# First chunks as fp32 on two other queues, loads ahead of the weights, and a new instruction order, in a windowed attention and highway kernel

## The chip, the cores and the metric

The kernel runs on one core of one Trainium2 chip. The metric is the time of one execution on the device in microseconds (us); a time "of runs" is a median over several executions, and a "span" is the length of one traced execution, some 1.7 us shorter than its run. A difference counts as a change if it is over 2%. The engines are named as the profile names them: PE is TensorE's matmuls and PEld its weight loads, DVE is VectorE, ACT ScalarE, POOL GpSimd, SP SyncE.

## The reference, cut to what matters

```python
# q, k, v: [4, 8, 768, 64] fp32; n_sink = 4, window = 128
scores = q @ k.transpose(0, 1, 3, 2) / sqrt(64)
keep = (column < n_sink) | (0 <= row - column < window)
a = softmax(where(keep, scores, -1e9)) @ v          # [4, 8, 768, 64]
x = a.transpose(0, 2, 1, 3).reshape(3072, 512)
H = maximum(x @ w_h, 0);  T = sigmoid(x @ w_t + b_t)
out = T * H + (1 - T) * x                           # [3072, 512] fp32
```

## The kernel before

The 3072 tokens are 24 blocks of 128, six to a batch. Block n needs query chunk n, key and value chunks n-1 (of its batch), n and n+1 (the chunks are cut 64 rows apart from the blocks), the four sink keys of its batch, and both weight matrices. Its steps have short names in one long list that fixes the order on every engine:

```python
"Tq": transpose of a query chunk (TensorE)     "tq"/"tqV": its copy out of PSUM (ScalarE / VectorE)
"Tk", "tk": the same for a key chunk           "S": scores, "x0_", "x1_": exponentials (ScalarE)
"m0_", "m1_": masks (VectorE)                  "sk", "es": sink scores and their exponentials
"A": the av matmuls                            "xh": division by the row sums (VectorE)
"X", "xT": transpose of x and its copy         "Mh", "Mt": x @ w_h, x @ w_t;  "u": tanh (ScalarE)
"d", "e", "o": the mix and the output (VectorE)
"fk": fills the sink tiles of batch 0 and the bias row (VectorE)
```

All loads of q, k, v and the weights are issued by GpSimd and cast from fp32 to fp16 on the way. The first lines of its queue, and the place where a later batch's sink keys are copied:

```python
        load_q(0); load_k(0); load_k(1)
        ...                                  # identity
        load_v(0)
        tri(mask, ...)  # x4, the masks
        load_q(1); load_v(1); load_k(2)
        load_w(moe_w_h, wh_sb)
        ...
        load_v(2); load_q(2); load_k(3)
        load_w(moe_w_t, wt_sb)
        load_v(3)
        ...                                  # then q, k, v of one block after the other
    def copy_T(m, g, eng=None):
        ...
        if g and m and m % NSC == 0 and m < NB:
            fill_ks(m // NSC, nc.gpsimd)     # two small copies of the sink keys
            sink_v(m // NSC, nc.gpsimd)
```

The softmax here doesn't subtract the row's maximum and nothing guards it: scores larger than these inputs give would overflow.

Of the kernel before, what the change touches and what calls it, by code (L numbers as in the profile page):

```python
# [20 lines left out]
def kernel(  # L21
# [18 lines left out]
    nc = tc.nc  # L40
# [85 lines left out]
    es_t = [const.tile([P, 2, P], FP16, tag=f"es{i}", name=f"es{i}") for i in range(2)]  # L126

    with tc.manual_schedule(engines={ENG.DVE}):
        nc.vector.memset(k_first[0:HP], 0.0)
        nc.vector.memset(v_ring[0][0:HP, 0:H * 65], 0.0)  # L130
        nc.vector.memset(warm, 0.0)
        nc.vector.memset(ident, 1.0)
        nc.vector.memset(ebias, _EXP_BIAS)
        nc.vector.memset(mask, 1.0)
        nc.vector.memset(bm, 1.0)
        for vt in v_ring:
            init_v(vt)
        nc.vector.memset(bt16, 0.0)
        nc.vector.memset(ones_row, 0.0)
        nc.vector.memset(ones_row[0:1, :], 1.0)  # L140
        for i in range(2):
            nc.vector.memset(ks_bd[i], 0.0)
            nc.vector.memset(vs_bd[i], 0.0)
            nc.vector.memset(es_t[i], 0.0)
# [11 lines left out]
    def load_w(w, sb):  # L156
        nc.gpsimd.dma_start(out=sb, in_=w.rearrange("(kc p) of -> p kc of", p=P))

    with tc.manual_schedule(engines={ENG.Pool, ENG.SP}):
        nc.sync.dma_start(out=bt32, in_=moe_b_t.unsqueeze(0))  # L160
        for b in range(B):
            nc.sync.dma_start(out=vs_dn[b], in_=v[b, :, 0:NSINK, :])
        load_q(0)
        load_k(0)
        load_k(1)
        nc.gpsimd.affine_select(
            out=ident, in_=ident, compare_op=ALU.is_equal, fill=0.0,
            base=0, pattern=[[-1, P]], channel_multiplier=1)
        load_v(0)
        tri(mask, slice(0, HP), 0, P, HP - 1, -1, 1)  # L170
        tri(mask, slice(HP, P), 0, P, 0, 1, -1)
        tri(mask, slice(0, HP), P, EW, 0, 1, -1)
        tri(mask, slice(HP, P), P, EW, -1, -1, 1)
        load_q(1)
        load_v(1)
        load_k(2)
        load_w(moe_w_h, wh_sb)
        nc.gpsimd.affine_select(
            out=bm, in_=bm, compare_op=ALU.is_ge, fill=0.0,
            base=0, pattern=[[-NSINK, H]], channel_multiplier=1)  # L180
        nc.gpsimd.affine_select(
            out=bm, in_=bm, compare_op=ALU.is_ge, fill=0.0,
            base=NSINK - 1, pattern=[[NSINK, H]], channel_multiplier=-1)
        load_v(2)
        load_q(2)
        load_k(3)
        load_w(moe_w_t, wt_sb)
        load_v(3)


    def more_masks():
        nc.vector.tensor_copy(out=mask0, in_=mask)
        nc.vector.memset(mask0[0:HP, 0:P], 0.0)
        nc.vector.memset(mask0[HP:HP + NSINK, 0:P], 1.0)
        nc.vector.memset(mask0[HP:P, P:EW], 0.0)
# [62 lines left out]
    def act_sink(n):  # L258
        es = es_t[(n if n < NSC else n // 2) % 2]
        bl = sink_blocks(n)  # L260
        nc.scalar.activation(out=es[0:NS4, 0:len(bl)], in_=sk_of.pop(n)[0:NS4, 0:len(bl)],
                             func=AF.Exp, bias=ebias[0:NS4], scale=SCALE)
        for t, m in enumerate(bl):
            es_of[m] = es[:, t, :]
# [38 lines left out]

    def pe_AB(n):
        av = av_ps.tile([P, 2, 4, P], FP32, tag="av", name="av")
        av_of[n] = av
# [98 lines left out]
    TS = 6  # L405
# [43 lines left out]
    def norm(n):  # L449
        dve_rec(n)  # L450
        dve_x(n)

    STEP = {
# [84 lines left out]
```

## Time and profile before

Three runs: 132.74 us median (132.39 to 134.89); the traced run took 130.48 us, with a span of 128.8.

| | busy us | share of the span |
|---|---|---|
| PE | 109.5 | 85% |
| DVE | 102.3 | 79% |
| ACT | 90.7 | 70% |
| POOL | 76.4 | 59% |

The view by stretches adds up each engine's busy time between two times. Columns: stretch in us, its length, then busy us (instructions) of PE, PEld, DVE, ACT, POOL, the granted TensorE clock, the DMA share and GB/s.

```profile
0.00:30.00 30.00, 19.88 (x288) 11.62 (x289) 15.38 (x71) 13.67 (x21) 24.19 (x38) 1.00 1.63 123
30.00:50.00 20.00, 18.09 (x366) 11.54 (x365) 16.15 (x33) 16.02 (x29) 18.12 (x24) 1.00 2.05 173
50.00:126.00 76.00, 71.56 (x1340) 45.43 (x1338) 70.77 (x130) 61.06 (x102) 34.12 (x42) 1.00 1.13 127
```

The reader is to see VectorE: 15.38 of the first 30 us, 16.15 of the next 20, and nearly all of the rest. With the work left as it is, the time can fall here only by what VectorE (and TensorE beside it) stands idle: 26.5 us of the span for VectorE.

### The profile page before, as it was taken

The numbers are of one execution on the slowest core, as the hardware profiler recorded it, in microseconds if no ns is written. First come the engines' busy times: TensorE is split into PE (matmuls) and PEld (weight loads), VectorE is DVE, ScalarE is ACT, GpSimd is POOL, SyncE is SP. The second block draws the span as 40 slices with busy tenths as digits, with TensorE's granted clock in tenths as the row PEclk, the third lists the DMA queues.
The fourth block names the chain that finished last, engine by engine and source line by source line (L and its number), as shares of the span: only waits on it lengthen the run. The fifth ranks groups of instructions, "written<-read, shape, count | busy, mean of one in ns | idle before, by whom it ended". The sixth has DMA issues, their size and how long they took to land.

```text
span 128.8 us, 4699 instructions
## 1 busy us (share of the span) xinstructions
PE 109.5 (85%) x1984; PEld 68.6 (53%) x1984; DVE 102.3 (79%) x232; ACT 90.7 (70%) x150; POOL 76.4 (59%) x102
## 2 busy tenths in 40 slices
PE   4841948979999769997999999999899999999830
PEld 1221735355676346665665665667466665665310
DVE  7618432548996939994999999989999999899990
ACT  3253626448989857999688879989689798893310
POOL 6998965788997898997869996846100000000000
PEclk9999999999999999999999999999999999999997
DMA  0999999999999999999999999999221022211142
GB/s 4 113 72 141 138 178 169 155 144 116 163 207 159 204 169 144 172 159 194 209 178 101 195 181 159 206 200 156 88 87 59 28 87 84 81 48 38 74 153 99
DMA packets 79702, 17.11 MB, mean 133 GB/s; under 512 B 75585, under 2 KB 76609, under 8 KB 79682
## 3 DMA queue, kind: packets, MB, share of 16 engines
q0 software_dynamic: 76064, 10.49, 122.1%
q1 hardware_dynamic: 3618, 6.33, 13.7%
q8 instruction: 15, 0.25, 0.8%
q14 instruction: 5, 0.04, 0.1%
HBM read 21.01 MB, written 6.29 MB: 212 GB/s over the span
## 4 chain that ended last, share of the span: by engine, by line
PE 66%; DVE 10%; POOL 8%; DMA 6%; ACT 4%; issue 4%; POOLq 0%; ACTq 0%
PE hps L377 14%; PE tps L364 13%; PE av L323 6%; DMA v<-in_v_dram 6%; PE av L312 6%; PE xtp L351 5%; PE sps L229 4%; PE sps L272 4%; PE sps L285 4%; PE sk L254 4%; PE tps L362 4%; PE av L329 3%; DVE dd L383 3%; DVE xh L342 2%; POOL v L104 2%
## 5 line engine op out<-in xcount | busy, mean ns | idle before, releaser
L290 ACT ACTIVATE e<-sps,ebias 128x768 f16<-128x768 f32 x48 | 41.3, 895 | 5.9 <-PE sps L285 5.8
L234 ACT COPY t<-sps 128x512 f16<-128x512 f16 x47 | 25.0, 583 | 12.7 <-PE sps L229 12.7
L298 DVE TENSOR_TENSOR e<-e,mask 128x768 f16<-128x768 f16 x48 | 26.0, 565 | 6.1 <-ACT e L290 5.6
L104 POOL DMA_DIRECT2D v<-in_v_dram x28 | 23.6, 841 | 8.1 <-DVE e L298 1.9
L377 PE MATMUL hps<-wh_sb,xT 128*128 128x512 f16 x96 | 25.5, 394 | 0.0
L364 PE MATMUL tps<-wt_sb,xT 128*128 128x512 f16 x96 | 24.6, 379 | 0.0
L97 POOL DMA_DIRECT2D ksd<-in_k_dram x27 | 23.2, 860 | 0.8 <-issue 0.5
L90 POOL DMA_DIRECT2D qsd<-in_q_dram x24 | 22.1, 921 | 2.2 <-DMA wt_sb<-in_moe_w_t_dram 1.3
L370 ACT ACTIVATE u<-tps 128x512 f16<-128x512 f32 x24 | 14.4, 599 | 9.2 <-PE tps L364 7.2
L389 DVE SCALAR_TENSOR_TENSOR ee<-u,dd 128x512 f16<-128x512 f16 x24 | 17.1, 714 | 0.4 <-ACT u L370 0.2
L383 DVE SCALAR_TENSOR_TENSOR dd<-hps,xh 128x512 f16<-128x512 f32 x24 | 16.5, 688 | 1.1 <-PE hps L377 1.0
L342 DVE TENSOR_TENSOR xh<-av,rec 128x512 f16<-128x512 f32 x24 | 16.6, 691 | 0.8
L395 DVE SCALAR_TENSOR_TENSOR otok<-xh,ee 128x512 f32<-128x512 f16 x24 | 16.6, 690 | 0.7
L364 PEld LDWEIGHTS <-xT 128*128 128x128 f16 x96 | 9.3, 97 | 11.7 <-issue 1.3
L312 PE MATMUL av<-v,e 64*64 64x66 f16 x384 | 11.2, 197 | 2.9 <-DMA v<-in_v_dram 2.1
L377 PEld LDWEIGHTS <-xT 128*128 128x128 f16 x96 | 9.5, 102 | 7.9 <-issue 1.6
L272 PE MATMUL sps<-t,t 64*128 64x128 f16 x192 | 12.6, 227 | 1.2 <-ACT t L234 1.2
L356 ACT COPY xT<-xtp 128x512 f16<-128x512 f16 x16 | 9.3, 583 | 3.3 <-PE xtp L351 3.2
L312 PEld LDWEIGHTS <-e 64*64 64x64 f16 x384 | 8.7, 111 | 4.6 <-DVE e L298 2.3
L337 DVE RECIPROCAL rec<-av 128x8 f32<-128x8 f32 x24 | 4.9, 205 | 7.8 <-PE av L329 6.5
L351 PE MATMUL xtp<-ident,xh 128*128 128x128 f16 x96 | 9.9, 227 | 1.3 <-DVE dd L383 0.8
L229 PE MATMUL sps<-ident,ksd 64*128 64x64 f16 x192 | 7.1, 196 | 4.5 <-DMA ksd<-in_k_dram 4.5
(61 smaller groups left out, 132.4 us busy)
## 6 DMA issues: line engine op xcount, KB each, us to landing
out_dram<-otok SPq DMA_DIRECT2D x24, 256.0 KB, 4.8
qsd<-in_q_dram POOLq DMA_DIRECT2D x24, 128.0 KB, 7.4
ksd<-in_k_dram POOLq DMA_DIRECT2D x20, 128.0 KB, 7.2
v<-in_v_dram POOLq DMA_DIRECT2D x20, 128.0 KB, 7.5
v<-in_v_dram POOLq DMA_DIRECT2D x8, 64.0 KB, 6.2
wh_sb<-in_moe_w_h_dram POOLq DMA_DIRECT2D x1, 512.0 KB, 8.1
wt_sb<-in_moe_w_t_dram POOLq DMA_DIRECT2D x1, 512.0 KB, 9.0
ksd<-in_k_dram POOLq DMA_DIRECT2D x7, 64.0 KB, 7.1
```

The lines of the kernel that those rows point to most:

```text
L90: nc.gpsimd.dma_start(out=qsd, in_=q[b, :, c * P:(c + 1) * P, :].transpose([1, 0, 2]))
L97: nc.gpsimd.dma_start(out=ksd[rows], in_=k[b, :, s0:s0 + nr, :].transpose([1, 0, 2]))
L104: nc.gpsimd.dma_start(out=vt[rows, :, 0:D], in_=v[b, :, s0:s0 + nr, :].transpose([1, 0, 2]))
L234: (eng or nc.scalar.copy)(out=t.rearrange("p a (h b) -> p h a b", b=HP), in_=t_view(s_tile(n, g)))
L272: nc.tensor.matmul(sps[:, hh, hl * EW:hl * EW + P], lhsT=kT[n][rows, hp, :], rhs=qT[n][rows, hp, :], start=True, stop=True)
L290: nc.scalar.activation(out=e.rearrange("p a b c -> p a (b c)"), in_=s_tile(n, g)[:, :, 0:2 * EW], func=AF.Exp, bias=ebias, scale=SCALE)
L298: nc.vector.tensor_tensor(out=ev, in0=ev, in1=m.unsqueeze(1).to_broadcast([P, 4, EW]), op=ALU.mult)
L312: nc.tensor.matmul(av[part, h // 4, h % 4, 0:_AVN], lhsT=e_at(n, h)[src, P:EW], rhs=vt[src, 65 * h:65 * h + _AVN], start=(h % 4 == 0), sto ...
L342: nc.vector.tensor_tensor(out=xh.rearrange("p (h d) -> p h d", d=D), in0=av_of.pop(n)[:, :, 0:D], in1=rec_of.pop(n).unsqueeze(2).to_broadc ...
L364: nc.tensor.matmul(tps, lhsT=xT[:, kc, :], rhs=wt_sb[:, kc, :], start=False, stop=(kc == NOC - 1))
L377: nc.tensor.matmul(hps, lhsT=xT[:, kc, :], rhs=wh_sb[:, kc, :], start=(kc == 0), stop=(kc == NOC - 1))
L383: nc.vector.scalar_tensor_tensor(out=dd, in0=h_of.pop(n), scalar=0.0, in1=xh_of[n], op0=ALU.max, op1=ALU.subtract)
```

## The change

Its intent is to have the queries and keys of blocks 0 to 4 and the values of blocks 0 and 1 on the chip before the weights (two matrices of 512 KB in fp16) take the DMA engines, and to use the wait for the weights for the transposes and sink scores of blocks 1 to 4. Five first loads go to SyncE and ScalarE as fp32, uncast, and are converted by VectorE and ScalarE. Cut to its core:

```diff
+        load_f32("q", 0, nc.sync)
+        load_f32("k", 0, nc.scalar)
+        load_f32("k", 1, nc.sync)
+        load_f32("v", 0, nc.scalar)
+        load_f32("v", 1, nc.sync)
         ...
-        load_q(0) load_k(0) load_k(1) ... load_v(0) tri x4 load_q(1) load_v(1) load_k(2)
-        load_w(moe_w_h, wh_sb) ... load_v(2) load_q(2) load_k(3) load_w(moe_w_t, wt_sb) load_v(3)
+        load_q(1) ... load_q(2) load_k(5) ... load_q(3) load_k(2) load_v(2) load_k(3)
+        tri x4  load_q(4) load_k(4)
+        load_w(moe_w_h, wh_sb) load_v(3) load_w(moe_w_t, wt_sb)
+        load_k(6) load_q(5) load_v(4) load_v(5) load_k(7) load_q(6) ...
-    es_t = [... for i in range(2)]
+    es_t = [... for i in range(4)]
     ORDER = """
-    Tq:0 Tk:0 tq:0 tk:0 Tk:1 tk:1 S:0 x0_:0 x1_:0 m0_:0 m1_:0 fk:0 Tk:2 Tq:1 tk:2 A:0 tq:1 xh:0
-    S:1 sk:1 x0_:1 X:0 xTV:0 x1_:1 m0_:1 es:1 m1_:1 A:1 Tq:2 xh:1 Tk:3 tq:2 tk:3 X:1 xT:1 S:2 ...
+    ckV:0 cq:0 ma:0 Tk:0 Tq:0 tk:0 ma:1 ck:1 tq:0 mc:0 Tk:1 tk:1 fk:0 S:0 x0_:0 cvV:0 x1_:0
+    mz0_:0 Tq:1 m0_:0 tq:1 Tq:2 m1_:0 tq:2 Tq:3 cvV:1 tq:3 sk:2 mz1_:0 Tk:2 es:2 Tk:5 tk:2 tkV:5
+    S:1 A:0 x0_:1 sk:1 x1_:1 xh:0 Tk:4 tk:4 m0_:1 Tk:3 es:1 m1_:1 Tq:4 tk:3 sk:3 tqV:4 es:3 sk:4
+    A:1 es:4 X:0 xh:1 S:2 ...
```

"ck", "cq", "cv" are conversions (V: on VectorE), "ma" clears the sink tiles, "mc" the bias rows, "mz0_", "mz1_" make the masks of a batch's first two blocks. The kernel before ran these clears ahead of the list (VectorE was done with them at 5.46 us) and the sink set-up "fk" behind the first block's masks; now the clears stand in the list, and they and "fk" come ahead of the masks. The order from block 20 on is new too, and one constant that says which score tile hosts a transpose goes from 6 to 8. The four sink tiles are needed by the new order: "es:4" now comes before the av of block 2, which still reads what "es:2" wrote, so with two tiles it would be overwritten (worked out from the list).

More of the change, by code (lines that the diff above doesn't have):

```diff
@@ L125, with load_f32, convert @@
     vs_dn = [const.tile([NS4, D], FP32, tag=f"vd{i}", name=f"vd{i}") for i in range(B)]
-    es_t = [const.tile([P, 2, P], FP16, tag=f"es{i}", name=f"es{i}") for i in range(2)]
+    es_t = [const.tile([P, 2, P], FP16, tag=f"es{i}", name=f"es{i}") for i in range(4)]
     with tc.manual_schedule(engines={ENG.DVE}):
+        nc.vector.memset(ident, 1.0)
+        nc.vector.memset(warm, 0.0)
+        nc.vector.memset(mask, 1.0)
+        nc.vector.memset(bm, 1.0)
+        nc.vector.memset(ebias, _EXP_BIAS)
         nc.vector.memset(k_first[0:HP], 0.0)
         nc.vector.memset(v_ring[0][0:HP, 0:H * 65], 0.0)
-        nc.vector.memset(warm, 0.0)
-        nc.vector.memset(ident, 1.0)
-        nc.vector.memset(ebias, _EXP_BIAS)
-        nc.vector.memset(mask, 1.0)
-        nc.vector.memset(bm, 1.0)
         for vt in v_ring:
             init_v(vt)
-        nc.vector.memset(bt16, 0.0)
-        nc.vector.memset(ones_row, 0.0)
-        nc.vector.memset(ones_row[0:1, :], 1.0)
-        for i in range(2):
-            nc.vector.memset(ks_bd[i], 0.0)
-            nc.vector.memset(vs_bd[i], 0.0)
-            nc.vector.memset(es_t[i], 0.0)
+    f32_of = {}
+    def load_f32(kind, n, eng):
+        t = const.tile([P, H, D], FP32, tag=f"{kind}f{n}", name=f"{kind}f{n}")
+        src = {"q": q, "k": k, "v": v}[kind]
+        for rows, b, s0 in ([(slice(0, P), 0, n * P)] if kind == "q" else chunk_parts(n)):
+            nr = rows.stop - rows.start
+            eng.dma_start(out=t[rows], in_=src[b, :, s0:s0 + nr, :].transpose([1, 0, 2]))
+        f32_of[kind, n] = t
+    def convert(kind, n, eng):
+        rows = slice(HP, P) if kind != "q" and n == 0 else slice(0, P)
+        if kind == "v":
+            dst = v_ring[n][:, 0:H * 65].rearrange("p (h e) -> p h e", e=65)[:, :, 0:D]
+        elif kind == "q":
+            dst = q_sd[n] = sd_pool.tile([P, H, D], FP16, tag="qsd", name="qsd")
+        else:
+            dst = k_sd[n] = k_first if n == 0 else sd_pool.tile([P, H, D], FP16, tag="ksd",
+                                                                name="ksd")
+        eng(out=dst[rows], in_=f32_of.pop((kind, n))[rows])
     def tri(t, rows, lo, hi, base, step, cm):
@@ L162 @@
             nc.sync.dma_start(out=vs_dn[b], in_=v[b, :, 0:NSINK, :])
-        load_q(0)
-        load_k(0)
-        load_k(1)
+        load_q(1)
         nc.gpsimd.affine_select(
@@ L168 @@
             base=0, pattern=[[-1, P]], channel_multiplier=1)
-        load_v(0)
-        tri(mask, slice(0, HP), 0, P, HP - 1, -1, 1)
-        tri(mask, slice(HP, P), 0, P, 0, 1, -1)
-        tri(mask, slice(0, HP), P, EW, 0, 1, -1)
-        tri(mask, slice(HP, P), P, EW, -1, -1, 1)
-        load_q(1)
-        load_v(1)
-        load_k(2)
-        load_w(moe_w_h, wh_sb)
+        load_q(2)
+        load_k(5)
         nc.gpsimd.affine_select(
@@ L183, with first_mask @@
             base=NSINK - 1, pattern=[[NSINK, H]], channel_multiplier=-1)
+        load_q(3)
+        load_k(2)
         load_v(2)
-        load_q(2)
         load_k(3)
-        load_w(moe_w_t, wt_sb)
-        load_v(3)
-    def more_masks():
+        tri(mask, slice(0, HP), 0, P, HP - 1, -1, 1)
+        tri(mask, slice(HP, P), 0, P, 0, 1, -1)
+        tri(mask, slice(0, HP), P, EW, 0, 1, -1)
+        tri(mask, slice(HP, P), P, EW, -1, -1, 1)
+        load_q(4)
+        load_k(4)
+        load_w(moe_w_h, wh_sb)
+        load_v(3)
+        load_w(moe_w_t, wt_sb)
+        load_k(6)
+        load_q(5)
+        load_v(4)
+        load_v(5)
+        load_k(7)
+        load_q(6)
+        load_v(8)
+        load_k(8)
+        load_q(7)
+        load_v(7)
+        load_v(6)
+    def first_mask(_):
         nc.vector.tensor_copy(out=mask0, in_=mask)
@@ L195, in more_masks, with second_mask, clear_sinks, bias_rows @@
         nc.vector.memset(mask0[HP:P, P:EW], 0.0)
+    def second_mask(_):
         nc.vector.tensor_copy(out=mask1, in_=mask)
         nc.vector.memset(mask1[HP:HP + NSINK, P:EW], 0.0)
+    def clear_sinks(i):
+        nc.vector.memset(ks_bd[i], 0.0)
+        nc.vector.memset(vs_bd[i], 0.0)
+        nc.vector.memset(es_t[i], 0.0)
+        nc.vector.memset(es_t[i + 2], 0.0)
+    def bias_rows(_):
+        nc.vector.memset(bt16, 0.0)
+        nc.vector.memset(ones_row, 0.0)
+        nc.vector.memset(ones_row[0:1, :], 1.0)
     def sink_ones():
@@ L258, in act_sink @@
     def act_sink(n):
-        es = es_t[(n if n < NSC else n // 2) % 2]
+        es = es_t[(n if n < NSC else n // 2) % 4]
         bl = sink_blocks(n)
@@ L302, in e_at, with av_tile @@
         return e_of[n, h // 4][:, h % 2, (h // 2) % 2, :]
+    def av_tile(n):
+        if n not in av_of:
+            av_of[n] = av_ps.tile([P, 2, 4, P], FP32, tag="av", name="av")
+        return av_of[n]
     def pe_AB(n):
-        av = av_ps.tile([P, 2, 4, P], FP32, tag="av", name="av")
-        av_of[n] = av
+        av = av_tile(n)
         nxt = v_ring[(n + 1) % NV]
@@ L403, in has_sink @@
         return 0 < n < NSC or on(n) and n % 2 == 1
-    TS = 6
+    TS = 8
     H0 = 4
@@ L451, in norm, with spare @@
         dve_x(n)
+    def spare(t):
+        nc.tensor.matmul(t, lhsT=warm[:, 0:P], rhs=warm, start=True, stop=True)
     STEP = {
@@ L462 @@
         "Mh": pe_Mh, "Mt": pe_Mt, "u": act_u, "d": dve_d, "e": dve_e, "o": dve_o,
-        "fk": first_sinks,
+        "fk": first_sinks, "mz0_": first_mask, "mz1_": second_mask, "ma": clear_sinks,
+        "mc": bias_rows,
+        "cq": lambda n: convert("q", n, nc.scalar.copy),
+        "ck": lambda n: convert("k", n, nc.scalar.copy),
+        "cv": lambda n: convert("v", n, nc.scalar.copy),
+        "cqV": lambda n: convert("q", n, nc.vector.tensor_copy),
+        "ckV": lambda n: convert("k", n, nc.vector.tensor_copy),
@@ L464 @@
+        "cvV": lambda n: convert("v", n, nc.vector.tensor_copy),
+        "wq": lambda n: spare(s_tile(("t", n, 0), 0)[:, 0, :]),
+        "wk": lambda n: spare(s_tile(("t", n, 1), 1)[:, 0, :]),
+        "wS": lambda n: spare(s_tile(n, 0)[:, 0, :]),
+        "wA": lambda n: spare(av_tile(n)[:, 0].rearrange("p a b -> p (a b)")),
     }
     ORDER = """
-    Tq:0 Tk:0 tq:0 tk:0 Tk:1 tk:1 S:0 x0_:0 x1_:0 m0_:0 m1_:0 fk:0 Tk:2 Tq:1 tk:2 A:0 tq:1 xh:0
-    S:1 sk:1 x0_:1 X:0 xTV:0 x1_:1 m0_:1 es:1 m1_:1 A:1 Tq:2 xh:1 Tk:3 tq:2 tk:3 X:1 xT:1 S:2
@@ L468 @@
-    sk:2 x0_:2 Mh:1 es:2 m0_:2 x1_:2 Mh:0 d:1 m1_:2 d:0 A:2 Tq:3 xh:2 Tk:4 tq:3 tk:4 S:3 X:2
-    x0_:3 Mt:1 xTV:2 x1_:3 m0_:3 sk:3 Tk:5 u:1 m1_:3 Tq:4 es:3 tkV:5 Mt:0 tq:4 e:1 sk:4 o:1 u:0
-    S:4 es:4 e:0 A:3 x0_:4 o:0 Mh:2 x1_:4 xh:3 Mt:2 tq:5 d:2 tk:6 m0_:4 sk:5 u:2 S:5 m1_:4 es:5
-    e:2 X:3 x0_:5 A:4 xTV:3 o:2 x1_:5 Mt:3 xh:4 tq:6 tk:7 m0_:5 Tq:7 u:3 X:4 tqV:7 S:6 xT:4
-    m1_:5 A:5 x0_:6 Mh:3 x1_:6 xh:5 Mt:4 tq:8 d:3 tk:8 m0_:6 S:7 u:4 m1_:6 e:3 sk:7 x0_:7 X:5
-    o:3 A:6 es:7 xTV:5 x1_:7 Mh:4 xh:6 tq:9 Mt:5 d:4 tk:9 m0_:7 X:6 u:5 m1_:7 S:8 xT:6 e:4 A:7
@@ L474 @@
-    x0_:8 o:4 Mh:5 x1_:8 xh:7 Mt:6 tq:10 d:5 tk:10 m0_:8 X:7 u:6 m1_:8 S:9 xT:7 e:5 A:8 x0_:9
-    o:5 sk:9 x1_:9 xh:8 Mh:6 es:9 m0_:9 tq:11 Mt:7 d:6 tk:11 m1_:9 X:8 e:6 u:7 S:10 xT:8 o:6 A:9
-    x0_:10 Mh:7 x1_:10 xh:9 Mt:8 tq:12 d:7 tk:12 m0_:10 X:9 u:8 m1_:10 S:11 xT:9 e:7 sk:11
-    x0_:11 o:7 A:10 es:11 m0_:11 x1_:11 Mh:8 xh:10 tq:13 Mt:9 d:8 tk:13 m1_:11 X:10 u:9 S:12
-    xTV:10 e:8 A:11 x0_:12 o:8 Mh:9 x1_:12 xh:11 Mt:10 tq:14 d:9 tk:14 m0_:12 X:11 u:10 m1_:12
-    S:13 xT:11 e:9 sk:13 x0_:13 o:9 A:12 es:13 m0_:13 Mh:10 x1_:13 xh:12 Mt:11 tq:15 d:10 tk:15
@@ L480 @@
-    m1_:13 X:12 u:11 S:14 xTV:12 e:10 A:13 x0_:14 o:10 Mh:11 x1_:14 xh:13 Mt:12 tq:16 d:11 tk:16
-    m0_:14 X:13 u:12 m1_:14 S:15 xT:13 e:11 sk:15 x0_:15 o:11 A:14 es:15 m0_:15 x1_:15 Mh:12
-    xh:14 tq:17 Mt:13 d:12 tk:17 m1_:15 X:14 u:13 e:12 S:16 xT:14 o:12 A:15 x0_:16 Mh:13 x1_:16
-    xh:15 Mt:14 tq:18 d:13 tk:18 m0_:16 X:15 u:14 m1_:16 S:17 xT:15 e:13 sk:17 x0_:17 o:13 A:16
-    es:17 m0_:17 x1_:17 Mh:14 xh:16 tq:19 Mt:15 d:14 tk:19 m1_:17 X:16 u:15 S:18 xTV:16 e:14
-    A:17 x0_:18 o:14 Mh:15 x1_:18 xh:17 Mt:16 tq:20 d:15 tk:20 m0_:18 X:17 u:16 m1_:18 S:19
@@ L486 @@
-    xT:17 e:15 sk:19 x0_:19 o:15 A:18 es:19 m0_:19 Mh:16 x1_:19 xh:18 Mt:17 tq:21 d:16 tk:21
-    m1_:19 X:18 u:17 S:20 xTV:18 e:16 A:19 x0_:20 o:16 Mh:17 x1_:20 xh:19 Mt:18 tq:22 d:17 tk:22
-    m0_:20 X:19 u:18 m1_:20 S:21 xT:19 e:17 A:20 x0_:21 o:17 sk:21 x1_:21 xh:20 Mh:18 es:21
-    m0_:21 tq:23 Mt:19 d:18 tk:23 m1_:21 X:20 u:19 e:18 S:22 xT:20 A:21 o:18 x1_:22 Mh:19 xh:21
-    x0_:22 Mt:20 tk:24 d:19 m0_:22 X:21 u:20 m1_:22 S:23 xT:21 e:19 A:22 x0_:23 o:19 sk:23 Mt:21
-    es:23 xh:22 x1_:23 m0_:23 Mh:20 u:21 m1_:23 X:22 d:20 A:23 xT:22 e:20 Mh:22 xh:23 Mh:21 d:22
@@ L492 @@
-    d:21 X:23 xT:23 o:20 Mt:22 e:21 Mh:23 o:21 u:22 e:22 Mt:23 d:23 o:22 u:23 e:23 o:23
+    ckV:0 cq:0 ma:0 Tk:0 Tq:0 tk:0 ma:1 ck:1 tq:0 mc:0 Tk:1 tk:1 fk:0 S:0 x0_:0 cvV:0 x1_:0
+    mz0_:0 Tq:1 m0_:0 tq:1 Tq:2 m1_:0 tq:2 Tq:3 cvV:1 tq:3 sk:2 mz1_:0 Tk:2 es:2 Tk:5 tk:2 tkV:5
+    S:1 A:0 x0_:1 sk:1 x1_:1 xh:0 Tk:4 tk:4 m0_:1 Tk:3 es:1 m1_:1 Tq:4 tk:3 sk:3 tqV:4 es:3 sk:4
+    A:1 es:4 X:0 xh:1 S:2 xT:0 x0_:2 Mh:0 x1_:2 m0_:2 X:1 d:0 S:3 xT:1 m1_:2 x0_:3 Mh:1 x1_:3
+    m0_:3 A:2 d:1 Mt:0 xh:2 m1_:3 X:2 u:0 S:4 xTV:2 e:0 A:3 x0_:4 o:0 Mt:2 x1_:4 xh:3 tq:5 Mt:1
@@ new lines @@
+    m0_:4 tk:6 m1_:4 u:2 S:5 u:1 e:1 sk:5 x0_:5 X:3 A:4 xTV:3 es:5 m0_:5 x1_:5 Mh:2 xh:4 tq:6
+    Mt:3 tk:7 d:2 m1_:5 X:4 u:3 e:2 S:6 xT:4 o:1 A:5 x0_:6 o:2 Mh:3 x1_:6 xh:5 Mt:4 tq:7 d:3
+    tk:8 m0_:6 X:5 u:4 m1_:6 S:7 xT:5 e:3 A:6 x0_:7 o:3 Mh:4 x1_:7 xh:6 Mt:5 tq:8 d:4 tk:9 m0_:7
+    Tq:9 u:5 sk:7 tqV:9 m1_:7 S:8 es:7 e:4 X:6 x0_:8 Mh:5 o:4 xT:6 m0_:8 A:7 tq:10 d:5 x1_:8
+    sk:9 xh:7 Mt:6 es:9 tk:10 m1_:8 X:7 e:5 u:6 S:9 xT:7 o:5 A:8 x0_:9 Mh:6 x1_:9 xh:8 Mt:7
+    tq:11 d:6 tk:11 m0_:9 X:8 u:7 m1_:9 S:10 xT:8 e:6 A:9 x0_:10 o:6 Mh:7 x1_:10 xh:9 Mt:8 tq:12
@@ new lines @@
+    d:7 tk:12 m0_:10 X:9 u:8 m1_:10 S:11 xT:9 e:7 sk:11 x0_:11 o:7 A:10 es:11 m0_:11 x1_:11 Mh:8
+    xh:10 tq:13 Mt:9 d:8 tk:13 m1_:11 X:10 u:9 S:12 xTV:10 e:8 A:11 x0_:12 o:8 Mh:9 x1_:12 xh:11
+    Mt:10 tq:14 d:9 tk:14 m0_:12 X:11 u:10 m1_:12 S:13 xT:11 e:9 sk:13 x0_:13 o:9 A:12 es:13
+    m0_:13 Mh:10 x1_:13 xh:12 Mt:11 tq:15 d:10 tk:15 m1_:13 X:12 u:11 S:14 xTV:12 e:10 A:13
+    x0_:14 o:10 Mh:11 x1_:14 xh:13 Mt:12 tq:16 d:11 tk:16 m0_:14 X:13 u:12 m1_:14 S:15 xT:13
+    e:11 sk:15 x0_:15 o:11 A:14 es:15 m0_:15 x1_:15 Mh:12 xh:14 tq:17 Mt:13 d:12 tk:17 m1_:15
@@ new lines @@
+    X:14 u:13 e:12 S:16 xT:14 o:12 A:15 x0_:16 Mh:13 x1_:16 xh:15 Mt:14 tq:18 d:13 tk:18 m0_:16
+    X:15 u:14 m1_:16 S:17 xT:15 e:13 sk:17 x0_:17 o:13 A:16 es:17 m0_:17 x1_:17 Mh:14 xh:16
+    tq:19 Mt:15 d:14 tk:19 m1_:17 X:16 u:15 S:18 xTV:16 e:14 A:17 x0_:18 o:14 Mh:15 x1_:18 xh:17
+    Mt:16 tq:20 d:15 tk:20 m0_:18 X:17 u:16 m1_:18 S:19 xT:17 e:15 sk:19 x0_:19 o:15 A:18 es:19
+    m0_:19 Mh:16 x1_:19 xh:18 Mt:17 tq:21 d:16 tk:21 m1_:19 X:18 u:17 S:20 xTV:18 e:16 A:19
+    x0_:20 o:16 Mh:17 x1_:20 xh:19 Mh:18 tq:22 d:17 tk:22 m0_:20 sk:21 m1_:20 S:21 es:21 d:18
@@ L493 @@
+    A:20 x0_:21 e:17 X:19 o:17 x1_:21 Mt:18 xTV:19 tq:23 xh:20 Mh:19 u:18 tk:23 m0_:21 X:20
+    m1_:21 xT:20 S:22 d:19 A:21 x1_:22 e:18 sk:23 x0_:22 xh:21 Mt:19 es:23 m0_:22 tk:24 Mt:20
+    m1_:22 u:19 o:18 X:21 u:20 e:19 S:23 xT:21 A:22 o:19 x0_:23 Mh:20 xh:22 x1_:23 Mh:21 d:20
+    m0_:23 Mt:21 d:21 m1_:23 X:22 u:21 xTV:22 A:23 e:20 Mh:22 xh:23 d:22 X:23 xT:23 o:20 Mt:22
+    e:21 Mh:23 o:21 u:22 e:22 Mt:23 d:23 o:22 u:23 e:23 o:23
     """
@@ L496 @@
         warm_up(8)
-        more_masks()
-        for n in range(3, AHEAD):
-            load_set(n)
         for step in ORDER.split():
```

## The prediction

> **What bounds the kernel now.** I read three views in this order: the strip of 40 slices on the page (where an engine is idle), the timeline of the first 26 us (why), and the chain that ended last (whether those waits set the end). The strip first; a slice is 128.8 / 40 = 3.22 us.
>
> ```profile
> PE   4841948979999769997999999999899999999830
> DVE  7618432548996939994999999989999999899990
> ...
> DMA  0999999999999999999999999999221022211142
> ```
>
> VectorE (DVE) has work for 1 to 8 tenths of the first ten slices, dips to 6 and 3 in slices 13 and 15, and stays near 9 after that; TensorE likewise. By stretch it is busy 19.85 of the first 35 us and 82.45 of the next 91. So the steady part is bound by VectorE and TensorE together, and what can be gained is the start: 15 us of idle VectorE, and the dip at 40 to 50 us (6.79 of 10 busy).
>
> The timeline of the start shows what the idle slices wait for. Columns: start in us, duration, engine, line, operation, count, and in brackets the idle time before it with what ended it.
>
> ```profile
> 8.78 0.78 POOL L157 DMA_DIRECT2D wh_sb<-in_moe_w_h_dram  x1
> 8.99 1.69 ACT L290 ACTIVATE e<-sps,ebias 128x768 f16<-128x768 f32 x2 [0.75 <-PE sps L285]
> ...
> 10.36 0.91 POOL L104 DMA_DIRECT2D v<-in_v_dram  x1 [0.30 <-issue]
> ...
> 12.29 0.40 PE L229 MATMUL sps<-ident,ksd 64*128 64x64 f16 x8 [3.25 <-DMA ksd<-in_k_dram]
> ...
> 17.98 0.65 PE L312 MATMUL av<-v,e 64*64 64x66 f16 x16 [2.07 <-DMA v<-in_v_dram]
> ...
> 22.50 3.07 PE L377 MATMUL hps<-wh_sb,xT 128*128 128x512 f16 x8
> ```
>
> Block 1 needs v chunk 2. Its load is issued at 10.36, behind the first weight matrix (8.78), and lands 7.5 us later; before the weights a load lands in 3.0 to 4.4 us. TensorE waits for key chunk 2 for 3.25 us and for v chunk 2 for 2.07 us. The eight H matmuls of blocks 0 and 1 at 22.5 still take about 0.43 us each, four times 0.86/4 = 0.215 us later on: TensorE has not sped up by then. The chain confirms that this start is on the path, and shows a second hole.
>
> ```profile
> 10.36 7.49 DMA v<-in_v_dram
> 17.98 0.65 PE av L312 x16
> ...
> 43.91 0.68 POOL v L104
> 44.59 0.27 issue
> 45.04 0.51 issue
> 46.06 0.62 PE sk L254 x8
> ```
>
> In the closer chain of 39 to 48 us, GpSimd's small copy of the next batch's sink keys (L243, 45.54 to 46.01) stands between those loads and the sink scores at 46.06. It was queued behind twelve blocks' loads, which are late because the whole queue is late. From 50 us on nothing waits long: 4.19 us a block (the av matmuls start at 50.78 for block 7 and 113.57 for block 22: 62.79 / 15).
>
> **What the Trainium skill says.** "DMA: Bandwidth & Descriptors", section "SWDGE vs HWDGE vs iDMA": a load that casts can only be issued by GpSimd; a plain one may come from SyncE or ScalarE. That is why the five new loads arrive as fp32 and need a conversion. The same page, "Issuing engines are not separate DMA queues": all queues share 16 DMA engines, and more issuers save only issue time. The trace agrees with the limit that matters: GpSimd takes 0.88 us to issue a load and starts only at 1.32, while SyncE issues at 0.81 and idles from 4.14. "SBUF — State Buffer", section "SBUF: two separate sides": while VectorE runs an fp32 copy in SBUF it locks GpSimd out of the descriptor writes. The trace has GpSimd loads released by VectorE operations (idle 1.9 us in 3 places); the new fp32 copies on VectorE are only three. "TensorE: Matmul & The Clock Gate", Part 1: the array runs at half rate until some 3.4 us of sustained activity. The 0.43 against 0.215 us above agree; the granted clock on the page reads 9 throughout and does not show it.
>
> **The change, part by part.**
>
> *First loads.* q0, k0, k1, v0, v1 go from GpSimd to SyncE and ScalarE, at 0.81 instead of 1.32 to 7.04. With the landing times of 3.0 us (64 KB) and 3.8 us (128 KB) of before, less what a cast-free queue may save, I take k0 and q0 at about 3.4, k1 at 4.3. Then ScalarE must finish its table load (1.28 us, now behind two issues: to about 3.5), convert q0 and k1 (0.58 us each, the mean of its 128x512 copy) and copy three transposed chunks (3 x 0.58). I get the first exponentials at about 7.2 instead of 8.99.
>
> *Masks.* They move behind seven loads: GpSimd does 7 x 0.88 + 0.33 + 0.5 from 1.32, then 1.21 for four triangles: together to about 9.7 with the longer first issue (1.07); before, 6.2. With the mask copies, 0.65, and two products, 1.1, block 0 is masked at about 11.5; the conversion of v1 follows, 0.5, and its av matmuls start at 12.1, against 12.83. So the earlier exponentials are mostly lost; this part alone gives 0.7 us.
>
> *Loads ahead of the weights.* q1 to q4, k2 to k5 and v2 are issued before the first weight matrix. At 0.88 each, k4, the last, is issued at about 10.6 and lands, 4.3 us later (as k2 did before), at 15. TensorE's order puts the transposes of k4, k3, q4 and the sink scores of blocks 3 and 4 ahead of block 1's av, so block 1 starts at about 17.2, against 17.98. But by then all transposes to q4 and k5 are done (before: to q1 and k2), and v2 waits for nobody. The weights follow: W_h issued at 11.5 plus the 8.1 of before lands at 19.6, W_t near 23.5 (before 16.9 and 22.0).
>
> *The next blocks*, from TensorE's new order with the durations of the trace (S 0.9 slow or 0.6 fast, av 1.3 or 1.0, Mh and Mt 0.86 to 1.1 fast): S2 and Mh0 at 20, S3 and Mh1 to 23, av2 at 23 to 24 (before 25.5), Mt0 to 25, S4 to 26.6, av3 at 26.6 (before 32.96), Mt2, Mt1, S5, then av4 at about 31.6, xh of block 4 done at 33.5 (before 39.2). v4 and q5 land, by the 0.95 us from landing to landing seen behind W_t before, at about 26, just in time.
>
> *What is owed.* At that point the new order has done one d, one e and two o fewer: 0.69 + 0.71 + 2 x 0.69 = 2.8 us of VectorE work. VectorE's own period without waits is 3.83 us a block (reciprocals at 51.67 and 55.50). From xh 4 to xh 9 the new order has five full blocks plus one copy, 5 x 3.83 + 0.4 = 19.5, and some 1.2 us of waits around the sink scores: xh 9 at about 54.2, against 61.8. Before spent 22.6 on this stretch with less work, since it had the hole at 45 us and idle times of 1.6 us and 1.1 us. In the new queue the copy of the sink keys is asked for later relative to the loads (sink scores of 7 come after the products of block 7), so that hole closes. One o is still owed at xh 9, 0.7 us, so about 6.9 us would be left; the order from there to block 19 is the same.
>
> *Added work.* VectorE gets k0, v0, v1 conversions (some 0.4 to 0.55 each, as its 0.42 us copy of the same size from PSUM), two clears (0.17 each) and one more transposed copy (0.42): about 2.2 us, all but 0.4 of it before 14 us, where it is waiting anyway. Rotating four instead of two es tiles only lets sink scores run ahead. The unused helpers for idle matmuls emit nothing: both kernels have the same 3970 rows on TensorE. The tail from block 20 on is reordered; I give that nothing.
>
> Sum: 6.9 us if each landing holds. I take off 1.9: the new start has several loads landing within 1 us of their use (k4, W_h, W_t, v4), and any one that is a microsecond late moves everything behind it. That leaves 5.0 us: 132.74 - 5.0 = 127.7 us.
>
> **The rivals.**
> 1. *The transfers only change place.* The DMA engines are busy at 9 tenths from slice 2 to slice 27, and all 24 blocks' data still come through them. Ahead of W_h there were seven loads and there will be fourteen (two of them halves). If these push W_h, W_t, v4 and q5 back by 7 x 0.95 = 6.7 us instead of the 3 I allowed, Mh0 would be at 24 and block 3's av at 31: a gain of 1 to 2 us, 131 us. For it: W_h took 8.1 us even then. Against it: GpSimd's issue, not the DMA engines, set the pace until 9 us (0.88 us a load, landing 0.9 us apart), and the five fp32 loads no longer pass through it.
> 2. *GpSimd and the masks become the bound of block 0.* If descriptors are held up by VectorE's copies and clears, the masks come at 11.5 and k4 at 17: gain 2 to 3 us, 130 us.
> 3. *TensorE stays slow for longer.* Waits for q3 and k4 (some 1.5 us each) could put off the full rate. Blocks 0 to 2 then cost 0.4 us more per av, and 0.86 per Mh: 2 us off the gain.
> 4. *Everything arrives as worked out*, with no delay: 6.9 us, 125.8 us.
>
> **Range and chances.** Rivals 1 and 2 together give about 131, rival 4 about 125.8, so the range is 125.3 to 131.0. Faster by over 2% means below 130.09, a gain of 2.65 us, about half of what I expect: 0.79. Within 2%: 0.18. Slower by over 2% would need a new wait of 8 us against what I count: 0.03.
>
> **What would show it.** Right: av of block 1 near 17, of block 3 near 27, of block 9 near 53; no wait of TensorE over 1 us for v chunk 2; no gap at the second batch's sink scores; H matmuls of block 0 at 0.215 us each. Wrong: av of block 0 after 14 (masks), a TensorE wait on W_h or v4 of several us between 18 and 28 (transfers), slow matmuls past 23, or a period over 4.3 us a block after block 9, which the change should not touch.

## The result, and the profile after

Four runs: 125.47 us median (124.94 to 125.97), against 132.56 (130.89 to 134.89) for four runs of the kernel before. The ratio is 0.9504, 95% interval 0.9403 to 0.9606: faster. (A ratio is taken over fast runs alone, a median over all runs, so the two do not quite agree.) The span is 123.2 us, 5.6 less than before.

The strip of 40 slices (here 3.08 us each) of the changed kernel, with the granted clock in tenths:

```profile
PE   5653589899999999999998999999899999999920
...
DVE  6299842679699999799999999799999999999980
...
PEclk9985555899999999999999999999999999999996
```

VectorE's dips in slices 13, 15 and 19 (6, 3 and 4 tenths before) are gone, though two later slices read 7, and TensorE is at 8 or 9 tenths from slice 9 to the last two. The stretches:

```profile
0.00:30.00 30.00, 22.31 (x376) 13.65 (x377) 19.88 (x80) 17.85 (x29) 24.75 (x38) 0.77 1.91 161
30.00:50.00 20.00, 20.00 (x398) 12.68 (x398) 18.47 (x37) 18.32 (x32) 18.50 (x24) 1.00 2.19 179
50.00:126.00 76.00, 66.69 (x1229) 41.99 (x1217) 66.29 (x123) 55.54 (x92) 29.31 (x37) 0.97 1.04 121
```

Idle time of VectorE is length less busy time (the last stretch ends with the span, at 128.8 and 123.2):

| stretch | idle before | idle after | less |
|---|---|---|---|
| 0 to 30 us | 14.62 | 10.12 | 4.5 |
| 30 to 50 us | 3.85 | 1.53 | 2.3 |
| 50 us to the end | 8.03 | 6.91 | 1.1 |

That is 7.9 us less idle time; VectorE's own work rose from 102.30 to 104.64, by 2.3; the difference is the 5.6 us of the spans.

The timeline answers to the lines shown for the start of before (columns as there):

```profile
11.38 0.78 POOL L171 DMA_DIRECT2D wh_sb<-in_moe_w_h_dram  x1
...
12.87 0.61 PE L270 MATMUL sps<-ident,ksd 64*128 64x64 f16 x16
...
19.82 0.65 PE L357 MATMUL av<-v,e 64*64 64x66 f16 x16
...
22.58 1.04 PE L422 MATMUL hps<-wh_sb,xT 128*128 128x512 f16 x4
```

The first weights are issued 2.6 us later, and none of these matmuls waits for a load. But block 1's av starts at 19.82, later than the 17.98 of before, and block 0's at 15.75 instead of 12.83. The start of the changed kernel is slower; it has more in hand. The av matmuls of some blocks show where it overtakes (start in us):

| block | 0 | 1 | 2 | 3 | 4 | 5 | 6 | 7 | 10 | 13 | 20 |
|---|---|---|---|---|---|---|---|---|---|---|---|
| before | 12.83 | 17.98 | 25.50 | 32.96 | 37.22 | 40.56 | 46.99 | 50.62 | 64.11 | 76.54 | 105.51 |
| after | 15.75 | 19.82 | 25.83 | 28.94 | 33.41 | 37.27 | 41.10 | 46.54 | 58.06 | 70.49 | 99.59 |

Before, 7.46 us pass from block 2 to 3, because ten transposes, scores and weight products stand between them; after, 3.11. Before, 6.43 pass from block 5 to 6, in the hole of the sink keys; after, 3.83. From block 10 to 20 both take 41.4 to 41.5.

Why the start is slower is in the chain that ended last (start, duration, what; its short pieces called "issue" are left out), in its first 17 us:

```profile
0.81 4.47 DMA kf<-in_k_dram
5.30 0.76 DVE k_first L158
6.18 0.28 DVE ks L230
6.53 0.49 DVE vs L231
...
10.51 0.61 DVE vs L166
11.16 0.49 DVE v L158
11.68 0.52 DVE mask L220
...
12.76 1.03 DVE e L339 x2
13.78 0.34 DVE v L158
14.12 0.41 DVE mask L226
...
14.71 0.43 DVE t L275
...
15.18 0.40 PE sps L313 x4
15.58 0.36 PE sps L326 x14
15.94 0.43 PE av L357 x11
```

It runs through VectorE: the fp32 key chunk lands at 5.28, its conversion takes 0.76, and then all clears, which the kernel before ran ahead of the list, and the sink set-up "fk", which it ran behind the first block's masks, stand ahead of the first mask. Behind the masked exponentials (done at 13.8) come the conversion of v1, the second mask and the copy of key chunk 5, and TensorE's order puts the scores of block 1, which wait for that copy, ahead of block 0's av. ScalarE's first exponentials start at 9.28 (8.99 before).

### The profile page after: what moved, and what is told of

It reads as the page before. It is cut to its first block, busy times and chain, and to the rows that moved or that the text cites. A ratio compares the mean times of both kernels' runs of the same rounds, so it can differ in the third digit from the quotient of the medians.

```text
span 123.2 us, 4699 instructions
## 1 busy us (share of the span) xinstructions
PE 109.0 (88%) x1984; PEld 68.3 (55%) x1984; DVE 104.6 (85%) x238; ACT 91.7 (74%) x151; POOL 72.6 (59%) x97
## 3 DMA queue, kind: packets, MB, share of 16 engines
q0 software_dynamic: 71888, 9.97, 125.3%
## 4 chain that ended last, share of the span: by engine, by line
PE 70%; DVE 18%; DMA 4%; issue 3%; ACT 2%; DVEq 0%; ACTq 0%
PE tps L409 14%; PE hps L422 13%; PE av L368 7%; PE av L357 6%; PE sps L270 5%; PE sk L295 5%; PE xtp L396 4%; PE sps L313 4%; PE sps L326 4%; PE tps L407 4%; DMA kf<-in_k_dram 4%; PE av L374 4%; DVE dd L428 3%; DVE ee L434 2%; DVE otok L440 2%
## 5 line engine op out<-in xcount | busy, mean ns | idle before, releaser
L339 DVE TENSOR_TENSOR e<-e,mask 128x768 f16<-128x768 f16 x48 | 25.4, 551 | 2.3 <-ACT e L331 1.8
L104 POOL DMA_DIRECT2D v<-in_v_dram x26 | 22.3, 861 | 3.9 <-DVE xh L387 1.4
L422 PE MATMUL hps<-wh_sb,xT 128*128 128x512 f16 x96 | 24.3, 379 | 0.0
L97 POOL DMA_DIRECT2D ksd<-in_k_dram x26 | 22.4, 872 | 2.6 <-DMA wh_sb<-in_moe_w_h_dram 1.9
L90 POOL DMA_DIRECT2D qsd<-in_q_dram x23 | 21.4, 930 | 1.5 <-POOLq L576 0.8
L440 DVE SCALAR_TENSOR_TENSOR otok<-xh,ee 128x512 f32<-128x512 f16 x24 | 17.2, 720 | 0.7
L368 PE MATMUL av<-v,e 128*128 128x66 f16 x192 | 10.9, 200 | 0.0
L396 PEld LDWEIGHTS <-xh 128*128 128x128 f16 x96 | 7.3, 100 | 6.5 <-DVE xh L387 1.5
```

The costliest lines, as they stand in the source:

```text
L90: nc.gpsimd.dma_start(out=qsd, in_=q[b, :, c * P:(c + 1) * P, :].transpose([1, 0, 2]))
L97: nc.gpsimd.dma_start(out=ksd[rows], in_=k[b, :, s0:s0 + nr, :].transpose([1, 0, 2]))
L104: nc.gpsimd.dma_start(out=vt[rows, :, 0:D], in_=v[b, :, s0:s0 + nr, :].transpose([1, 0, 2]))
L339: nc.vector.tensor_tensor(out=ev, in0=ev, in1=m.unsqueeze(1).to_broadcast([P, 4, EW]), op=ALU.mult)
L396: nc.tensor.transpose(xtp[:, j, :], xh[:, j * P:(j + 1) * P], ident)
L422: nc.tensor.matmul(hps, lhsT=xT[:, kc, :], rhs=wh_sb[:, kc, :], start=(kc == 0), stop=(kc == NOC - 1))
```

## The experiments

The kernel before spreads, 127.8 to 134.9 us, and a run over 1.5% above a kernel's fastest is called slow and left out of a ratio, so its fast runs are a low selection of a wide spread. One run below checks this: the kernel before against itself read 1.011. I therefore give medians beside ratios, and take nothing under 1.5% as shown.

**order_only.** All loads as before, no conversions, new order.

```diff
-        (the new loads, fp32 first)
+        (the loads of before, all cast by GpSimd)
-    ckV:0 cq:0 ... ck:1 ... cvV:0 ... cvV:1       # conversions out of the new order
```

> The changed kernel with all loads put back as they were before (five first loads cast by GpSimd, weights behind k2 and k3) and no conversions; the new instruction order is kept. Theory L (the gain comes from the data being there before the weights, so that transposes and sink scores of blocks 1 to 4 fill the start): the new order then waits for q3 and k5, which landed at 23.8 and 27.5 in the kernel before; block 0's av moves from 15.8 to about 28, the time to 134 us or more. Rival O (the new order alone is the gain): about 126 us.

Measured: 139.71 us median (before 131.06), ratio 1.074 (1.062 to 1.086). Block 0's av starts at 29.69. The waits of its TensorE (what waited for what: us in total, times, longest):

```profile
PE sps L270 <- DMA qsd<-in_q_dram: 13.5, 2, 8.6
PE sps L270 <- DMA ksd<-in_k_dram: 3.8, 2, 2.5
```

The new order alone loses 8.7 us; the rival falls.

**weights_early.** The fp32 first loads kept, the other loads in the order of before.

```diff
-        load_q(1) load_q(2) load_k(5) load_q(3) load_k(2) load_v(2) load_k(3) tri load_q(4) load_k(4) load_w(w_h) ...
+        tri load_q(1) load_k(2) load_w(w_h) load_v(2) load_q(2) load_k(3) load_w(w_t) load_v(3) ...
```

> The changed kernel, fp32 first loads kept, but GpSimd's other loads in the order of before: W_h behind k2, W_t behind k3, masks early. Theory L: k5 lands at about 23 instead of 10.9, block 0's av starts near 24 instead of 15.8, total 131 to 134 us, most of the gain gone. Rival F (the early fp32 first loads are the gain): about 126 us.

Measured: 135.96 us, ratio 1.045 (1.034 to 1.056); block 0's av at 25.37, TensorE waits 9.4 us for queries. I expected 131 to 134: it is worse than the kernel before, not just without the gain. The new order needs the new load order; that the five early loads carry the gain is refuted in this setting.

**fp32_only.** The kernel before with the five fp32 loads and conversions only.

```diff
+        load_f32("q", 0, nc.sync)  ...  load_f32("v", 1, nc.sync)
-        load_q(0) load_k(0) load_k(1) load_v(0) load_v(1)
-    Tq:0 Tk:0 tq:0 tk:0 ...
+    ckV:0 cq:0 Tq:0 Tk:0 tq:0 tk:0 ck:1 ...
```

> The kernel before with only the fp32 first loads on SyncE and ScalarE and their conversions; its own order and load order. GpSimd's queue is five loads (about 4.3 us) shorter, so v2 should land near 13.5 instead of 17.9. Theory L: the work of blocks 1 to 4 is still stacked behind the weights, so only part arrives: 129.5 to 131.5 us. Rival F: 126 to 127 us. Rival O: 132.5 us, nothing.

Measured: 128.34 us (128.05 to 128.92), ratio 0.988 (0.978 to 0.998), 2.7 us by medians. Block 1's av starts at 16.54 (17.98), block 3's at 31.97 (32.96), and from block 5 to 6 pass 5.76 us (6.43): a shorter GpSimd queue helps at both places, by about 1 and 0.7 us. The median is somewhat lower than I expected; the ratio is under the 1.5% that I take as shown. One sign for later: block 0's av starts at 12.09 here, where the new order is not used.

**cast_first.** The changed kernel with the five loads cast by GpSimd, ahead of the rest.

```diff
-        load_f32("q", 0, nc.sync)  ...  load_f32("v", 1, nc.sync)
+        load_q(0) load_k(0) load_k(1) load_v(0) load_v(1)     # ahead of load_q(1)
-    ckV:0 cq:0 ... ck:1 ... cvV:0 ... cvV:1
```

> The changed kernel with the five first loads cast by GpSimd at the head of its queue, no conversions; everything else kept. All later loads are issued some 4.3 us later: masks ready near 14, k4 lands near 20 instead of 16.3, block 1's av near 22.5 instead of 19.8. Theory L: 127.5 to 128.5 us, most of the gain stays. Rival F: 131 to 132.5 us.

Measured: 127.61 us, ratio 0.985 (0.970 to 1.000); block 0's av at 17.20, block 1's at 22.05, 2.2 us behind the changed kernel. By medians 3.5 us of the gain stay without fp32 loads, as theory L said, though the ratio's interval reaches 1.000.

**loads_only.** All new loads and conversions, the old order.

```diff
+        (fp32 first loads and the whole new load order)
+    ckV:0 cq:0 Tq:0 Tk:0 ...                              # otherwise the order of before
```

> The kernel before with the fp32 first loads, their conversions and the whole new load order, but its own instruction order. It closes the square with fp32_only, weights_early and the changed kernel. Theory LO (load order and instruction order only work together): v2 lands near 14, so block 1's av starts near 17, but the transposes and sink scores of blocks 2 to 4 still stand behind it: 127.5 to 129.5 us, no better than fp32_only (128.3). Rival L (the loads alone are the gain): 125 to 126.5 us.

Measured: 129.65 us (128.34 to 131.03) against 131.25, ratio 0.995 (0.987 to 1.003). Loads alone, without the order, are no better than fp32_only. So the square reads, in medians: old loads and old order 131.1 to 131.3; new loads, old order 129.65; old loads, new order 139.71; both 126.16 (below). The new order needs the new loads, and the new loads show no gain without the new order.

**after_again, filler, sinks_later, tail_old** ran on one chip.

> The changed kernel again, as the yardstick of this call: 125 to 126 us.

The changed kernel again: 126.16 us (125.02 to 126.82), the kernel before 131.34, ratio 0.9644 (0.957 to 0.972). The gain is 5.2 us by medians.

```diff
     # filler: idle matmuls in TensorE's waits
-    Tk:1 tk:1 ... S:0 ... Tq:1 ... Tq:2 ... Tq:3 ... S:1 A:0
+    wk:1 wk:1 Tk:1 tk:1 ... wS:0 S:0 ... wq:1 wq:1 Tq:1 ... wq:2 Tq:2 ... wq:3 wq:3 Tq:3 ... wS:1 wS:1 S:1 wA:0 A:0
```

> The changed kernel with eleven idle matmuls (about 0.43 us each while slow) put into the waits of TensorE between 5 and 15 us, through the helpers that the change defines and does not use. Theory C (TensorE's slow clock, which lasts to about 22 us, is on the path of blocks 0 to 2): the full rate comes by about 12 us and the total falls by 1 to 2.5 us, to 123 to 124.5. Rival D (VectorE's clears and masks and the landing of k4 at 16.3 hold the start): no change, 125 to 126, or 0.5 us worse.

Measured: 125.35 us (124.43 to 126.83), ratio 0.954 (0.947 to 0.961), its interval overlapping that of after_again. The full rate came earlier: matmuls shrink from about 19.1 us on, instead of about 23 in after_again. But the idle matmuls ran at 0.43 us and pushed block 0's av to 17.54 and block 1's to 21.37, and block 2's starts at 26.39, against 26.14. What the earlier rate gives, the fillers take; whether a better placed filler would pay stays open.

```diff
     # sinks_later: sink set-up behind the first block's masks
-    ... mc:0 Tk:1 tk:1 fk:0 S:0 ... cvV:1 tq:3 sk:2 mz1_:0 Tk:2 es:2 Tk:5 tk:2 tkV:5 S:1 A:0 x0_:1 sk:1
+    ... Tk:1 tk:1 S:0 ... cvV:1 tq:3 mz1_:0 Tk:2 Tk:5 tk:2 tkV:5 fk:0 mc:0 S:1 A:0 x0_:1 sk:1 sk:2
```

> The changed kernel with VectorE's sink set-up (fk) and bias rows (mc), 2.7 us of work, moved from ahead of the first mask to behind the conversion of v1 and the copy of k5, and the sink scores of block 2 moved behind block 0's av. Theory D (VectorE's queue holds block 0): block 0's av starts near 13 instead of 15.8, block 1's near 18.8 instead of 19.8 (k4 lands at 16.3), total 0.5 to 1.5 us lower. Rival C: no change.

Its result was wrong: with mc behind fk the bias rows were cleared after they had been filled. The instructions and their waits are the same as in a correct one, so its times may be read: 124.99 us, ratio 0.957 (0.951 to 0.962). VectorE now reaches the mask before GpSimd has made it:

```profile
10.13 0.21 DVE L220 COPY mask<-mask 128x192 f16<-128x192 f16 x1 [1.73 <-POOL mask L161]
```

Block 0's av starts at 15.00 instead of 15.75 (I expected 13): behind the masks it waits in TensorE's own order, where the query chunk 3 (wait of 1.14 us) and the key chunk 2 come first. So VectorE's queue was the first of several bounds on the start.

> The changed kernel with the order of before from block 20's av on. In both traces some 20.2 us pass from block 20's av to the last store, so theory: no change, within 0.4 us. Rival T (the new tail is part of the gain): 0.8 us or more slower.

The diff: the order from block 20 on put back. Measured: 125.59 us, ratio 0.961 (0.954 to 0.968), no difference from after_again. The new tail has no measurable part in the gain.

**sinks_fixed.** As sinks_later, with mc behind cvV:0 and ahead of fk.

```diff
-    ... cvV:0 x1_:0 ... tkV:5 fk:0 mc:0 S:1
+    ... cvV:0 mc:0 x1_:0 ... tkV:5 fk:0 S:1
```

> As sinks_later, but with the bias rows cleared before they are filled, so the result must be correct now. If VectorE's queue holds the start: block 0's av near 15, block 2's near 24.2, and 0.5 to 1.5 us less than the changed kernel (ratio to the kernel before 0.005 to 0.01 lower than the changed kernel's 0.964). Rival: no difference from the changed kernel.

Measured: correct, 124.60 us (123.74 to 125.72), ratio 0.960 (0.953 to 0.966) against a kernel before of 131.25. It is the fastest median, 1.6 us under after_again; the ratio (0.960 against 0.964) is inside the intervals, and its traced span, 123.2, equals the changed kernel's. It was run at another time. Block 0's av starts at 14.76, as expected, but block 2's at 25.43 instead of 24.2 (25.83 in the changed kernel): of the 1.0 us won at block 0, 0.4 is left two blocks later. No gain in the total is shown.

**before_again.** The kernel before, unchanged, for a second trace.

> The kernel before once more, for a second trace: its runs spread over 127.8 to 134.9 us, the changed kernel's over 124.9 to 126.8. If the spread comes from when TensorE gets its full rate, the H matmuls of blocks 1 and 0 differ between this trace and the first (0.43 us each there) and the difference is made by 26 us; if it comes from single waits later on (0.8 us at block 9 in the first trace), the start agrees within 0.5 us and the difference appears after 40 us.

Measured: 131.28 us (130.47 to 131.36); ratio 1.011 (1.006 to 1.017) to itself, the bias named above. The start agrees with the first trace within 0.5 us (block 2's av at 24.99 and 25.50, block 3's at 32.69 and 32.96). The difference comes later, from block 6 to 7: 5.30 us here, 3.63 there. Its timeline:

```profile
46.59 0.62 PE L254 MATMUL sk<-t,ks 128*128 128x128 f16 x8 [2.08 <-POOL ks L243]
...
48.01 1.89 PE L377 MATMUL hps<-wh_sb,xT 128*128 128x512 f16 x4
...
50.12 1.68 PE L364 MATMUL tps<-wt_sb,xT 128*128 128x512 f16 x4
```

After a wait of 2.08 us for the sink keys the products take 1.89 and 1.68 us a group instead of 1.03, and the granted clock of that slice reads 5 tenths: TensorE lost its full rate for some 3.6 us (48.0 to 51.6). In the first trace the same wait was 1.7 us and the rate was kept. So the same hole costs a different amount from run to run. Neither trace points to the first 26 us as the source of the spread.

**before_ks_dve.** One word changed in the kernel before.

```diff
-            fill_ks(m // NSC, nc.gpsimd)
+            fill_ks(m // NSC, nc.vector)
```

> The kernel before with the small copy of the later batches' sink keys on VectorE instead of GpSimd, where it stood behind the loads until 46 us. If that hole was worth what the prediction gave it (about 2 us of VectorE's 3.2 idle us at 40 to 50): 1.5 to 2.5 us faster than the kernel before. Rival: the work that was held is only moved to the next block (blocks 5 to 7 took 10.1 us before and 9.3 after the change), so less than 1 us.

Measured: 128.59 us (127.46 to 131.54) against 131.25, ratio 0.988 (0.980 to 0.996); the kernel before read 1.011 against itself. VectorE makes the copy at 34.69, and the scores no longer wait (first line: the kernel before; second: this run):

```profile
46.06 0.62 PE L254 MATMUL sk<-t,ks 128*128 128x128 f16 x8 [1.72 <-POOL ks L243]
43.57 0.62 PE L254 MATMUL sk<-t,ks 128*128 128x128 f16 x8
```

From block 5 to 6 pass 4.48 us instead of 6.43 (6.63 in before_again), and from 6 to 7 3.62. The hole is worth 2.0 us in the traces and 2.7 by medians; the ratio alone would be under the 1.5% that I take as shown, the closed wait is what shows it.

Not run: the five fp32 loads and this one word together, in the old order. An estimate from the two traces: block 5's av at 39.58 (fp32_only), 8.10 us from there to block 7 and 12.94 more to block 10 (before_ks_dve) put block 10's av at 60.6, against 64.11 before and 58.06 in the changed kernel. So over half of the gain may be had without the new order; this is open.

## Why the prediction was right or wrong

The time, 125.47 us, lies inside the range of 125.3 to 131.0, at its lower edge, and the change is faster by over 2%, as held most likely. The gain expected as 5.0 us was 7.1 by medians, 5.2 in after_again, and 5.6 in the two traces. The kernel before alone moves by several us between runs, so how far 5.0 was too small is not settled. Of the prediction's own signs, the av of blocks 1, 3 and 9 came at 19.8, 28.9 and 53.8 instead of 17, 27 and 53; the others for being right held (no wait for v chunk 2, no gap at the second batch's sink scores, H matmuls of block 0 at full rate), and one sign of being wrong came true: block 0's av starts after 14, at 15.75.

*Bound and place.* Right. VectorE's idle time fell by 4.5 us in the first 30 us and 2.3 in the next 20; blocks 10 to 20 take the same time in both kernels. Some readings were not exact: the strip does not "stay near 9" past slice 15 (slice 19 reads 4, at the wait of 0.8 us in block 9's av); 50.78 and 113.57 are pieces of the chain, the av of these blocks start at 50.62 and 113.40 (the period stays 4.19); and both kernels have 1984 matmuls and 1984 weight loads, not 3970. The GpSimd loads "released by VectorE operations" stood behind mask products (L298), not fp32 copies. In the changed kernel GpSimd's issue beside the first fp32 conversion took 0.89 us, like its neighbours, so the lock that the prediction names does not show there.

*The second hole.* Right, and shown in the traces: before_ks_dve closes it alone and gains 2.0 us there, 2.7 by medians. In the changed kernel GpSimd copies these keys at 41.1, about 3 us before the scores at 43.99.

*First loads.* Wrong in size. I took 3.4 us for the first key chunk and 7.2 for the first exponentials. It landed at 5.28 and the exponentials began at 9.28. I had used the landing times of before, when GpSimd's queue was nearly alone; with five fp32 loads beside it, the second key chunk took 5.1 us from issue to landing, the v chunks 6.8 and 7.2, and GpSimd's first seven loads 7.0 to 7.3 (key chunk 4, for which I had carried over 4.3, took 5.8). cast_first shows that the fp32 loads do this: without them GpSimd's loads of 128 KB that are issued before 8.5 us land in 3.7 to 5.0 us.

*Masks.* The step that failed: "block 0 is masked at about 11.5 ... its av matmuls start at 12.1". GpSimd made the masks at 9.68, as worked out. But VectorE, in order, first did the clears and the sink set-up: 6.18 to 11.12 in the chain. Of these 4.9 us I had counted only the two added clears (0.34), as work in time "where it is waiting anyway"; that the new order moves all the others ahead of the masks I had overlooked. The mask copy began at 11.68, and block 0 was masked at 13.8 instead of 11.5. Another 2 us went by up to the av at 15.75, in VectorE's next three operations and in block 1's scores, which TensorE's order puts first; I had put only the conversion of v1 there. sinks_later shows the first bound: with the sink set-up behind the masks VectorE waits for GpSimd instead, and the av starts earlier, though by 0.75 us only, as queries and keys come next. fp32_only fits this: with the fp32 loads but the order of before, its av starts at 12.09.

*Loads ahead of the weights.* Right in kind. The weights landed at 19.2 and 22.4 (predicted 19.6 and 23.5); the blocks came later than predicted, by less and less: block 1 at 19.8 (17.2), block 3 at 28.9 (26.6), the division of block 4 done at 35.4 (33.5), that of block 9 at 55.8 (54.2). order_only and weights_early show that the new order without this load order loses 8.7 and 4.9 us by medians, loads_only that the loads without the order show no gain.

*The 1.9 us taken off* for late landings was a guess about the wrong thing. TensorE's longest direct wait for a load in the changed kernel is 0.6 us, for a query chunk. Instead the division of block 9 came 1.6 us later than worked out, behind a slow start that I had not foreseen. That the two are of one size, and 5.0 so near to 5.6, is luck. How much of the 1.6 us the slow start itself cost is not shown: sinks_fixed starts block 0's av 1.0 us earlier and has 0.4 of it left at block 9 (53.41 against 53.81).

*Added work* was 2.2 us, measured 2.34 (the conversion of the first key chunk took 0.76 us here and 0.42 in fp32_only; why is not shown). *The tail* was given nothing, and tail_old agrees.

*Rivals.* The first (transfers only change place) did not happen: the weights came 0.4 and 1.1 us earlier than they were put. The second named the right symptom, a late first block, with the wrong engine. The third (slow for longer than before) did not happen either: TensorE is slow to about 22 us (the granted clock reads 5 tenths in slices 4 to 7), but before it was slow to about 25. Four H matmuls take 1.04 us at 22.58, where the eight of before took 3.07 at 22.50. filler moved the full rate further forward and left the cost of the slow stretch undecided.

## What to carry to other kernels

Here loads moved forward paid only with an instruction order that had work for what they brought, and the new order only with its loads there: change both, and test each alone. Read the start engine by engine in queue order: work that "fits into idle time" still delays whatever stands behind it in the same queue. A small operation of a later stage does not belong in a queue that is full of load issues: here one word, which engine copies the sink keys, was worth 2 us in the traces.

## What the Trainium skill lacked or had wrong

- "TensorE: Matmul & The Clock Gate", Part 1, ties the return to half rate to an idle window of about 3.4 us (and, in another kernel, to frequent short pauses). In before_again TensorE lost it after a single wait of 2.08 us (H products 1.89 us a group instead of 1.03); in another run of the same kernel a wait of 1.7 us did not do it.
- The same page warns that clock events in traces are unreliable. The runs agree and give the case: in two traces of the changed kernel the granted clock reads 5 tenths in slices 4 to 7 in one and 9 in the other, while block 1's av matmuls take 0.65 us a group in both.
- "DMA: Bandwidth & Descriptors", section "Issuing engines are not separate DMA queues", is right that all queues share the engines, but gives no figure for what a second queue does to the landing of the first. Here GpSimd's loads of 128 KB went from 3.6 to 4.4 us to 7.0 to 7.3 us at the start, and an fp32 chunk on SyncE took 5.1 us. What the second queue won is bytes: from 3 to 6 us the engines moved 193 GB/s, against 105 before and 98 in cast_first.
- The same section calls the issue time usually small relative to the DMA. That holds here (0.7 us against landings of 4.5 to 6.8 us on ScalarE's queue), but it is time of the issuing engine: ScalarE's two issues put its table load back from 0.81 to 2.25 us, though the fp32 queries came later still.
